# One tuned transformer block on one core: wider loads, a sigmoid from exp and ln, and a maximum subtracted on another engine

## Chip, cores, metric

The kernel runs on one NeuronCore of a Trainium2 chip. The metric is the device time of one execution in microseconds (us). Each kernel is executed several times; the median is quoted, with the lowest and highest run. One execution of each kernel is profiled; its span is some 2 us shorter than its device time.

Every run also lists the mean clock that was granted to TensorE. In this case that column matters: 0.993 of full speed over a span of some 244 us means one stretch of 3.4 us at half clock (3.4 x 0.5 / 244 = 0.7%), as in the profiled run of before (clock 0.50 from 27.69 to 31.10 us), 0.986 two of them. I call such a stretch a **slow window**, and a run with 0.998 or more a **full-clock run**. A run's state, fast or slow, goes by its time. All means below are of runs of state fast; three runs of before that counted as slow (247.36, 248.15 and 249.84 us, at a mean clock of 0.985, 0.978 and 0.972) are left out.

## The reference

A block with adaptive layer norm: six modulation vectors from silu(c), a sliding-window attention (32 heads of 16, eight keys at distance 0, 2, ... 14), and a gated feed-forward.

```python
mod = silu(c) @ w_mod                      # c: 1x512, w_mod: 512x3072 -> sa, ca, ga, sb, cb, gb
h = layernorm(x) * (1 + ca) + sa           # x: 2048x512, bf16
q, k, v = split(h @ wqkv)                  # 512x1536
logits = einsum(q, k[idx]) * Dh**-0.5      # idx = pos - 2*(0..7); masked below 0
o = softmax(logits) @ v[idx]
x = x + ga * (o @ wo)
h = layernorm(x) * (1 + cb) + sb
x = x + gb * ((gelu(h @ w_gate) * (h @ w_up)) @ w_down)     # Df = 1792
```

## The kernel before

The tokens go in five groups (256, 256, 512, 512, 512). Each group has a first normalization, the q, k, v projections, the attention and the feed-forward. The program does not list its instructions in their final order. It declares operations with an engine, an assumed duration, tiles read and written, and a priority; a plan then simulates the engines and fixes the order of every engine. A change of one assumed duration or of one dependence can therefore move instructions that have nothing to do with it.

```python
def start(o):                              # in the plan: can o be placed yet?
    at = max([p.end - ... for p in o.pre], default=0.0)
    for t in o.tiles:
        if t.tag is not None and t not in seen:
            before = self.seqs[t.seq][t.at - 1] if t.at else None
            if before is not None and before not in seen and before not in o.tiles:
                return None                # the tile ahead in the sequence has not been placed
            ...                            # cut
```

The parts that the change touches (cut, in the kernel's own words):

```python
early = T("hh", [P, 2, SG], BF16, "early", "early")
wide = T("hh", [P, 2, SG], BF16, "wide", "early")       # same sequence as wm2 below
...
wm01 = [T("vR", [P, 4, 2, D // 2], BF16, "wm01", "early") for _ in range(2)]
wm2 = [T("hh", [P, 2, D], BF16, "wm2", "early") for _ in range(2)]
...
load_x(0, 2, -1000)
load_wm01(0)                               # shift and scale, 4 loads of 256 KB, rows of 512 B
load_wm01(1)
load_wqkv(0, -998.65)                      # wq, wk, wv: two loads each
load_wqkv(1, -997.5)
load_wqkv(2, L["wv"])
...
act(0.2, lambda: nc.scalar.activation(out=scT[:], in_=c_ps[:], func=ACT.Silu), r=[c_ps], w=[scT], pri=-990,
    table="silu")
dve(0.34, lambda: nc.vector.tensor_copy(out=wide.t[:, 0, :]..., in_=_ap(scT[:], [[1, 4], [0, P]])),
    r=[scT], w=[(wide, 0)], pri=-950)      # "the spread copy": silu(c) over 512 columns
...
if not onact:                              # inverse root of a group's variance: VectorE add, GpSimd power
    dve(0.09, lambda ...: nc.vector.tensor_scalar_add(out=rstd[:], in0=mv[:, :, 1], scalar1=EPS), ...)
    invsqrt(rstd, p)
elif g:                                    # or Ln and Exp on ScalarE, for groups in LNACT = (0, 1)
    act(0.45, lambda ...: rsqrt_act(rstd[:], mv[:, :, 1]), r=[mv, eps1], w=[rstd], pri=p - 1000, table="exp")
...
dve(us, ... Lb[:, 0, :] = max(Lb[:, 0, :], Lb[:, 1, :]))           # maximum over the eight keys
dve(us, ... Lb[0:64, 1, :] = max(Lb[0:64, 0, :], Lb[64:128, 0, :]))
dve(us, ... Lb[0:32, 0, :] = max(Lb[0:32, 1, :], Lb[32:64, 1, :]))
def sub_max():                             # TensorE adds -max to the logits in PSUM
    for t in LT:
        nc.tensor.matmul(t[:], lhsT=NB[:], rhs=_ap(Lb[:, 0, :], [[0, 2 // nb], [1, n]]), start=False, stop=True, ...)
pe(MM * nb, sub_max, r=[NB, Lb], w=LT, pri=p)
```

Of the kernel before, what the change touches and what calls it, by code (L numbers as in the profile page):

```python
# [9 lines left out]
ALU = mybir.AluOpType  # L10
# [188 lines left out]
LNACT = (0, 1)  # L199
SECOND = ()  # L200
MERGE = (3, 4)
FMERGE = 0
CUT = 384
# [26 lines left out]
def kernel(  # L230
# [59 lines left out]
    eps1 = ctile([P, 1], F32, "eps1")  # L290
    M = ctile([P, H], BF16, "Mph")
# [24 lines left out]
    def consts_dve():  # L316
        nc.vector.memset(warm(), 0.0)
        nc.vector.memset(one1[:], 1.0)
        nc.vector.memset(neghalf[:], -0.5)
        nc.vector.memset(onecol[:], 1.0)  # L320
        nc.vector.memset(eps1[:], EPS)

# [29 lines left out]
    dve(0.6, consts_dve, w=[(early, 0), one1, neghalf, onecol, eps1], pri=-1000)  # L352
# [26 lines left out]
    wm01 = [T("vR", [P, 4, 2, D // 2], BF16, "wm01", "early") for _ in range(2)]  # L379
# [32 lines left out]
    def load_wm01(i):  # L412
        for half in range(2):
            lo = half * D + i * (D // 2)
            dma(262e3, lambda half=half, lo=lo: nc.sync.dma_start(  # L415
                out=wm01[i][:, :, half, :], in_=w_mod[:, lo:lo + D // 2].rearrange("(t p) n -> p t n", p=P)),
                w=[(wm01[i], half)], pri=-999 + 0.5 * i + 0.1 * half, bw=385e3)

    def load_wqkv(b, p):
        for i in range(2):  # L420
            dma(262e3, lambda i=i: nc.sync.dma_start(
                out=wqkv[b][:, 2 * i:2 * i + 2, :],
                in_=A_wqkv[2 * i * P:2 * (i + 1) * P, b * D:(b + 1) * D].rearrange("(o p) n -> p o n", o=2)),
                w=[(wqkv[b], k) for k in range(2 * i, 2 * i + 2)], pri=p + 0.25 * i)

    load_wm01(0)
    load_wm01(1)
# [33 lines left out]
    def c_cols():  # L461
        for t in range(4):
# [5 lines left out]
    act(0.2, lambda: nc.scalar.activation(out=scT[:], in_=c_ps[:], func=ACT.Silu), r=[c_ps], w=[scT], pri=-990,  # L468
        table="silu")
    dve(0.34, lambda: nc.vector.tensor_copy(out=wide.t[:, 0, :].rearrange("p (t n) -> p t n", n=P),  # L470
                                            in_=_ap(scT[:], [[1, 4], [0, P]])), r=[scT], w=[(wide, 0)], pri=-950)
# [19 lines left out]
    def mod_first(src, p, after):  # L491
        parts = []
        for i2, chs in enumerate(((0, 1), (2, 3))):
# [4 lines left out]
            def cols(n=n, mps=mps, src=src[i2]):  # L498
                for half in range(2):
                    for i in range(n):  # L500
                        col = mps[:, half * n + i:half * n + i + 1]
                        for kt in range(4):
                            nc.tensor.matmul(col, lhsT=src[:, kt, half, i * P:(i + 1) * P],
# [4 lines left out]
            pe(0.25 * n, cols, r=[src[i2], scT, ident, onecol] + (after if i2 else []), w=[mps], pri=p)  # L508
# [95 lines left out]
    def ln1(g, dst, p):  # L604
        xns = []
        tok0, n = GROUPS[g]
        for half in range(n // 256):
# [7 lines left out]
            for i in range(2):  # L615
                dve(0.6, lambda i=i, st=st, tok=tok: nc.vector.bn_stats(out=st[:, i, :], in_=xrow(tok + P * i)),  # L616
                    r=[xkey(tok + P * i)], w=[(st, i)], pri=p)
                dve(0.081, lambda i=i, st=st, mv=mv: nc.vector.bn_aggr(out=mv[:, i, :], in_=st[:, i, :]),
                    r=[(st, i)], w=[(mv, i)], pri=p)
# [86 lines left out]
    def emit_attention(g):  # L706
# [78 lines left out]
        for b in range(nb):  # L785
# [5 lines left out]
        dve(us, lambda: nc.vector.tensor_tensor(out=Lb[0:64, 1, :], in0=Lb[0:64, 0, :], in1=Lb[64:128, 0, :],  # L791
                                                op=ALU.max), r=[Lb], w=[Lb], pri=p)
        dve(us, lambda: nc.vector.tensor_tensor(out=Lb[0:32, 0, :], in0=Lb[0:32, 1, :], in1=Lb[32:64, 1, :],
                                                op=ALU.max), r=[Lb], w=[Lb], pri=p)

        def sub_max():
            for t in LT:
                nc.tensor.matmul(t[:], lhsT=NB[:], rhs=_ap(Lb[:, 0, :], [[0, 2 // nb], [1, n]]), start=False, stop=True,  # L798
                                 skip_group_check=True)
# [209 lines left out]
```

## Time and profile before

| | before |
|---|---|
| median of the first 3 runs | 246.07 us (245.77 to 246.77) |
| span of the profiled run | 243.9 us, mean clock 0.993 |
| TensorE busy | 235.2 us, 96% |

In the profile, PE is TensorE, PEld its weight loads, DVE VectorE, ACT ScalarE, POOL GpSimd, SPq the queue of SyncE, which issues the loads. A line of a timeline has start, duration, engine, source line, operation, output and inputs, the count of merged instructions, and in brackets the idle time just before with what ended it. The prediction below shows the lines of before.

```profile
5.27 1.32 SPq L421 DMA_DIRECT2D wk<-in_A_wqkv_dram  x2
6.64 1.36 SPq L397 DMA_DIRECT2D wm<-in_w_mod_dram  x2
8.05 1.62 SPq L421 DMA_DIRECT2D wv<-in_A_wqkv_dram  x2
10.05 2.06 SPq L374 DMA_DIRECT2D x_sg<-in_A_x_dram  x3
```

The third part of the modulation weights (wm, 512 KB, not needed before 16 us) goes ahead of wv and of the rows of the later groups.

```profile
17.15 2.46 DVE L616 BATCH_NORM_STATS2 st<-x_sg 128x6 f32<-128x512 bf16 x4
...
22.25 0.72 DVE L532 TENSOR_SCALAR xn<-x_sg,mv,rstd 128x512 bf16<-128x512 bf16 x2
```

### The profile page before, as it was taken

The page shows a single profiled execution, that of the slowest core. Times are in us where ns is not written, and L with a number is a line of the kernel's source. Part 1 is how long each engine was busy: PE and PEld are TensorE (multiplying, and loading weights), DVE is VectorE, ACT ScalarE, POOL GpSimd, SP SyncE. Part 2 cuts the span into 40 slices and gives each one's busy share as a digit, 9 for nine tenths or more (in the row PEclk, how much of TensorE's full clock was granted, in tenths as well). Part 3 has the DMA queues.
Part 4 walks back from the last instruction along what each step waited for, and adds up shares of the span by engine and source line. Part 5 has one row for each costly group of instructions (what it writes and reads, how often), then busy time and mean ns, then how long its engine had stood idle before and what let it go on. Part 6 is the DMA issues. An engine that isn't in the chain of part 4 may idle for free.

```text
span 243.9 us, 4176 instructions
## 1 busy us (share of the span) xinstructions
PE 235.2 (96%) x1572; PEld 126.6 (52%) x1590; DVE 158.5 (65%) x302; ACT 159.5 (65%) x293; POOL 14.8 (6%) x37
## 2 busy tenths in 40 slices
PE   7899699999999999999999999999999999999994
PEld 2688355557665446755444444444444444444443
DVE  3589949829999499993699896299356222222222
ACT  5295687689788769388967748745767902666400
POOL 7002220010001000020000002000002000000000
PEclk9999799999999999999999999999999999999999
DMA  6999999999940309804117602210004010100011
GB/s 179 363 360 304 310 248 379 218 306 209 213 84 6 80 7 256 177 11 79 43 32 187 134 0 55 56 43 26 0 1 81 8 36 7 43 0 3 0 43 43
DMA packets 36533, 28.23 MB, mean 116 GB/s; under 512 B 11041, under 2 KB 35362, under 8 KB 36514
## 3 DMA queue, kind: packets, MB, share of 16 engines
q1 hardware_dynamic: 36512, 27.97, 45.8%
q8 instruction: 12, 0.20, 0.3%
q14 instruction: 7, 0.06, 0.1%
q10 hardware_dynamic: 2, 0.00, 0.0%
HBM read 21.40 MB, written 4.21 MB: 105 GB/s over the span
## 4 chain that ended last, share of the span: by engine, by line
PE 87%; DVE 6%; DMA 2%; ACT 2%; SPq 1%; issue 1%; DVEq 0%
PE g_ps L919 20%; PE u_ps L919 20%; PE y_ps L945 19%; PE qkv_ps L673 14%; PE x_ps L878 6%; PE o_ps L853 3%; PE LT L768 3%; DMA wm<-in_w_mod_dram 2%; DVE st L616 2%; DVE pq L756 2%; ACT hT L547 1%; PE LT L798 1%; PE ss L813 1%; SPq L415 1%; DVE x_sg L953 1%
## 5 line engine op out<-in xcount | busy, mean ns | idle before, releaser
L919 PE MATMUL g_ps<-h2T,Wg 128*128 128x512 bf16 (+1 forms) x280 | 57.7, 337 | 0.0
L919 PE MATMUL u_ps<-h2T,Wu 128*128 128x512 bf16 (+1 forms) x280 | 57.7, 337 | 0.0
L945 PE MATMUL y_ps<-WdP,hht 128*128 128x512 bf16 (+2 forms) x230 | 50.1, 366 | 0.4
L928 ACT ACTIVATE gl<-g_ps 128x512 bf16<-128x512 f32 x56 | 33.6, 600 | 25.6 <-PE g_ps L919 19.8
L932 DVE TENSOR_TENSOR hht<-gl,ub 128x512 bf16<-128x512 bf16 x56 | 23.2, 420 | 33.0 <-ACT ub L931 32.7
L931 ACT CAST ub<-u_ps 128x512 bf16<-128x512 f32 x56 | 32.8, 586 | 14.9 <-PE u_ps L919 14.8
L919 PEld LDWEIGHTS <-Wg 128*128 128x128 bf16 x280 | 27.1, 98 | 23.3 <-issue 1.7
L919 PEld LDWEIGHTS <-Wu 128*128 128x128 bf16 x280 | 27.1, 98 | 22.1 <-issue 1.5
L756 DVE TENSOR_TENSOR pq<-qT,kT 128x2048 bf16<-128x2048 bf16 x32 | 37.5, 1215 | 0.1
L945 PEld LDWEIGHTS <-hht 128*128 128x128 bf16 x238 | 22.8, 98 | 25.7
L953 DVE TENSOR_TENSOR x_sg<-y_ps,x_sg 128x512 bf16<-128x512 f32 (+2 forms) x17 | 10.8, 657 | 29.1 <-PE y_ps L945 29.1
L834 DVE TENSOR_TENSOR pv<-e,vR 128x2048 bf16<-128x2048 bf16 x24 | 28.3, 1217 | 0.1
L537 POOL TENSOR_TENSOR rstd<-rstd,neghalf 128x2 f32<-128x2 f32 x14 | 10.5, 756 | 169.8 <-DVE rstd L893 108.5
L673 PE MATMUL qkv_ps<-hT,wq 128*128 128x512 bf16 (+1 forms) x79 | 17.0, 348 | 0.2
L673 PE MATMUL qkv_ps<-hT,wk 128*128 128x512 bf16 (+1 forms) x78 | 16.8, 346 | 0.2 <-issue 0.2
L673 PE MATMUL qkv_ps<-hT,wv 128*128 128x512 bf16 (+1 forms) x79 | 15.2, 337 | 0.2 <-DMA wv<-in_A_wqkv_dram 0.2
L878 PE MATMUL x_ps<-woP,oT 128*128 128x512 bf16 x60 | 14.6, 379 | 0.2
L885 ACT ACTIVATE xn<-x_sg 128x512 bf16<-128x512 bf16 x16 | 10.0, 630 | 5.9 <-DVE x_sg L882 5.6
L696 ACT CAST kT<-qkv_ps 128x512 bf16<-128x512 f32 x16 | 9.4, 591 | 4.7 <-PE qkv_ps L673 3.6
L673 PEld LDWEIGHTS <-wq 128*128 128x128 bf16 x80 | 8.7, 115 | 6.8 <-issue 2.9
L616 DVE BATCH_NORM_STATS2 st<-x_sg 128x6 f32<-128x512 bf16 x16 | 10.4, 678 | 2.6 <-DMA x_sg<-in_A_x_dram 2.6
L696 ACT CAST qT<-qkv_ps 128x512 bf16<-128x512 f32 x16 | 9.4, 592 | 3.9 <-PE qkv_ps L673 3.7
(92 smaller groups left out, 215.6 us busy)
## 6 DMA issues: line engine op xcount, KB each, us to landing
vR<-scr SPq DMA_DIRECT2D x24, 260.0 KB, 4.9
vR<-scr SPq DMA_DIRECT2D x8, 264.0 KB, 9.5
wm<-in_w_mod_dram SPq DMA_DIRECT2D x8, 256.0 KB, 6.0
out_dram<-x_sg SPq DMA_DIRECT2D x15, 128.0 KB, 1.7
Wg<-in_B_w_gate_dram SPq DMA_DIRECT2D x2, 896.0 KB, 10.0
scr<-vT SPq DMA_DIRECT2D x7, 256.0 KB, 7.1
Wu<-in_B_w_up_dram SPq DMA_DIRECT2D x2, 896.0 KB, 8.5
WdP<-in_B_w_down_dram SPq DMA_DIRECT2D x2, 896.0 KB, 9.9
```

What stands on the lines that cost most here:

```text
L616: dve(0.6, lambda i=i, st=st, tok=tok: nc.vector.bn_stats(out=st[:, i, :], in_=xrow(tok + P * i)), r=[xkey(tok + P * i)], w=[(st, i)], pri=p)
L673: nc.tensor.matmul(shaped(ps[:, jl, :], g, XB1), lhsT=wqkv[b][:, dt, j + jl:D:4], rhs=columns(hT[g], g, dt, XB1), start=(dt == 0 and (jl = ...
L696: act(act_us(SG), lambda dst=dst, ps=ps: nc.scalar.copy(out=dst(), in_=ps[:]), r=[ps], w=w, pri=p)
L756: dve(1.145, lambda j=j, wg=wg, no=no, t=pq[m]: nc.vector.tensor_tensor(out=t[:], in0=_ap(q[g][:, j, :], [[0, no], [1, n]]), in1=_ap(kT[:, ...
L834: dve(1.145, lambda jj=jj, jl=jl, wg=wg, t=pv[m]: nc.vector.tensor_tensor(out=t[:], in0=_ap(e[:, wg, :], [[0, 4], [1, n]]), in1=vR[g][jj][ ...
L878: nc.tensor.matmul(x1_ps[:], lhsT=oT[:, j, c4 * P:(c4 + 1) * P], rhs=woP[:, j, :], start=(j == 0), stop=(j == 3))
L919: nc.tensor.matmul(shaped(ps[:, f, :], g, XB2), lhsT=Wt[:, dt, ft * P:(ft + 1) * P], rhs=columns(h2[g], g, dt, XB2), start=(dt == 0), stop ...
L928: act(act_us(SG), lambda gl=gl, ps=gu[0]: nc.scalar.activation(out=gl[:], in_=flat(ps), func=ACT.Gelu_apprx_tanh), r=[gu[0]], w=[gl], pri= ...
L931: act(act_us(SG), lambda ub=ub, ps=gu[1]: nc.scalar.copy(out=ub[:], in_=flat(ps)), r=[gu[1]], w=[ub], pri=p)
L932: dve(0.339, lambda gl=gl, ub=ub, ht=hh[u // 2], u=u: nc.vector.tensor_tensor(out=ht[:, u % 2, :], in0=gl[:], in1=ub[:], op=ALU.mult), r=[ ...
L945: nc.tensor.matmul(y_ps[:], lhsT=hh[u // 2][:, u % 2, f * n + c4 * P:f * n + (c4 + 1) * P], rhs=WdP[:, ft, lo_d:hi_d], start=(ft == 0), st ...
L953: dve(0.07 + nd * 1.041e-3, lambda y_row=y_row, y_ps=y_ps: nc.vector.tensor_tensor(out=y_row(), in0=y_ps[:], in1=y_row(), op=ALU.add), r=[ ...
```

## The change

Its intent: the first projection waits for the shift and scale weights, so they come in one load with rows four times as long; wq, wk and wv come in one load each; silu is computed from exp and ln, which share one activation table with the inverse roots; the first tiles' statistics are aggregated at once; group 2's inverse root moves to ScalarE; the last group's maximum is subtracted by VectorE instead of TensorE. The spread copy (silu(c) over 512 columns) moves behind the first hT tile. Cut to its core:

```diff
-LNACT = (0, 1)
+LNACT = (0, 1, 2)
+DVEMAX = (4,)
 ...
-    wm01 = [T("vR", [P, 4, 2, D // 2], BF16, "wm01", "early") for _ in range(2)]
+    wm01 = T("vR", [P, 4, 2 * D], BF16, "wm01", "early")
 ...
-    def load_wm01(i): ...                 # four loads, cut
+    dma(1049e3, lambda: nc.sync.dma_start(out=wm01[:], in_=w_mod[:, 0:2 * D].rearrange("(t p) n -> p t n", p=P)),
+        w=[wm01], pri=-999, bw=390e3)
     def load_wqkv(b, p):
-        for i in range(2):
-            dma(262e3, ...)                # cut
+        dma(524e3, lambda: nc.sync.dma_start(
+            out=wqkv[b][:], in_=A_wqkv[:, b * D:(b + 1) * D].rearrange("(o p) n -> p o n", p=P)), w=[wqkv[b]], pri=p)
 ...
-    act(0.2, lambda: nc.scalar.activation(out=scT[:], in_=c_ps[:], func=ACT.Silu), r=[c_ps], w=[scT], pri=-990,
-        table="silu")
-    dve(0.34, lambda: nc.vector.tensor_copy(out=wide.t[:, 0, :]..., in_=_ap(scT[:], ...)), r=[scT], w=[(wide, 0)], pri=-950)
+    def sigmoid():
+        nc.scalar.activation(out=sig[:], in_=c_ps[:], func=ACT.Exp, scale=-1.0)
+        nc.scalar.activation(out=sig[:], in_=sig[:], func=ACT.Ln, bias=one128[:])
+        nc.scalar.activation(out=sig[:], in_=sig[:], func=ACT.Exp, scale=-1.0)
+    act(0.5, sigmoid, r=[c_ps, one128], w=[sig], pri=-990, table="exp")
+    dve(0.15, lambda: nc.vector.tensor_tensor(out=scT[:], in0=c_ps[:], in1=sig[:], op=ALU.mult), ...)
 ...
+                if g == 0:                 # statistics and aggregation as one operation
+                    dve(0.75, lambda stats=stats, aggr=aggr: (stats(), aggr()), ...)
 ...
+        if g in DVEMAX:
+            dve(us, lambda: most(top[0:64, :], Lb[0:64, 0, :], Lb[64:128, 0, :]), ...)
+            dve(4 * us, spread, r=[top], w=[all4], pri=p)      # the last step four times, once for each 32 partitions
+            for b, t in enumerate(LT):
+                dve(..., lambda t=t: nc.vector.tensor_tensor(out=t[:], in0=t[:], in1=_ap(all4[:], ...), op=ALU.subtract), ...)
 ...
         if g == 0:
             mod_keep(mod0, -969)
+            dve(0.34, lambda: nc.vector.tensor_copy(out=wide.t[:, 0, :]..., in_=_ap(scT[:], ...)), r=[scT, hT[0]], w=[(wide, 0)],
+                pri=-950)
```

More of the change, by code (lines that the diff above doesn't have):

```diff
@@ L290 @@
     eps1 = ctile([P, 1], F32, "eps1")
+    one128 = ctile([P, 1], F32, "one128")
     M = ctile([P, H], BF16, "Mph")
@@ L321, in consts_dve @@
         nc.vector.memset(eps1[:], EPS)
+        nc.vector.memset(one128[:], 1.0)
     def consts_ident():
@@ L350, in consts_late @@
                                     fill=NEG, base=-8 * wg - 6, channel_multiplier=2)
-    dve(0.6, consts_dve, w=[(early, 0), one1, neghalf, onecol, eps1], pri=-1000)
+    dve(0.6, consts_dve, w=[(early, 0), one1, neghalf, onecol, eps1, one128], pri=-1000)
     gp(1.0, consts_ident, w=[ident], pri=-1000)
@@ L410 @@
     load_x(0, 2, -1000)
-    def load_wm01(i):
-        for half in range(2):
-            lo = half * D + i * (D // 2)
-            dma(262e3, lambda half=half, lo=lo: nc.sync.dma_start(
-                out=wm01[i][:, :, half, :], in_=w_mod[:, lo:lo + D // 2].rearrange("(t p) n -> p t n", p=P)),
-                w=[(wm01[i], half)], pri=-999 + 0.5 * i + 0.1 * half, bw=385e3)
-    def load_wqkv(b, p):
-        for i in range(2):
-            dma(262e3, lambda i=i: nc.sync.dma_start(
-                out=wqkv[b][:, 2 * i:2 * i + 2, :],
-                in_=A_wqkv[2 * i * P:2 * (i + 1) * P, b * D:(b + 1) * D].rearrange("(o p) n -> p o n", o=2)),
-                w=[(wqkv[b], k) for k in range(2 * i, 2 * i + 2)], pri=p + 0.25 * i)
-    load_wm01(0)
-    load_wm01(1)
+    dma(1049e3, lambda: nc.sync.dma_start(out=wm01[:], in_=w_mod[:, 0:2 * D].rearrange("(t p) n -> p t n", p=P)),
+        w=[wm01], pri=-999, bw=390e3)
+    def load_wqkv(b, p):
+        dma(524e3, lambda: nc.sync.dma_start(
+            out=wqkv[b][:], in_=A_wqkv[:, b * D:(b + 1) * D].rearrange("(o p) n -> p o n", p=P)), w=[wqkv[b]], pri=p)
     load_wqkv(0, -998.65)
@@ L467 @@
     keep_warm(PRI["warm"][1], [c_ps], -989)
-    act(0.2, lambda: nc.scalar.activation(out=scT[:], in_=c_ps[:], func=ACT.Silu), r=[c_ps], w=[scT], pri=-990,
-        table="silu")
-    dve(0.34, lambda: nc.vector.tensor_copy(out=wide.t[:, 0, :].rearrange("p (t n) -> p t n", n=P),
-                                            in_=_ap(scT[:], [[1, 4], [0, P]])), r=[scT], w=[(wide, 0)], pri=-950)
+    sig = ctile([P, 4], F32, "sig")
+    def sigmoid():
[3 more added lines that the diff above has]
+    act(0.5, sigmoid, r=[c_ps, one128], w=[sig], pri=-990, table="exp")
+    dve(0.15, lambda: nc.vector.tensor_tensor(out=scT[:], in0=c_ps[:], in1=sig[:], op=ALU.mult), r=[c_ps, sig],
+        w=[scT], pri=-2000)
     def mod_cols(src0, k0, src1, k1, p, off):
@@ L496, in mod_first, with cols @@
             mps = T("psB", [P, 2 * n], F32, "modT_ps", "mod")
-            def cols(n=n, mps=mps, src=src[i2]):
+            def cols(n=n, mps=mps, first=chs[0] * P):
                 for half in range(2):
@@ L502, in cols @@
                         for kt in range(4):
-                            nc.tensor.matmul(col, lhsT=src[:, kt, half, i * P:(i + 1) * P],
+                            nc.tensor.matmul(col, lhsT=src[:, kt, half * D + first + i * P:half * D + first + (i + 1) * P],
                                              rhs=scT[:, kt:kt + 1], start=(kt == 0), stop=(kt == 3 and half == 0))
@@ L506, in cols @@
                             nc.tensor.matmul(col, lhsT=ident[:], rhs=onecol[:], start=False, stop=True)
-            pe(0.25 * n, cols, r=[src[i2], scT, ident, onecol] + (after if i2 else []), w=[mps], pri=p)
+            pe(0.25 * n, cols, r=[src, scT, ident, onecol] + (after if i2 else []), w=[mps], pri=p)
             parts.append((chs[0], n, mps))
@@ L615, in ln1 @@
             for i in range(2):
-                dve(0.6, lambda i=i, st=st, tok=tok: nc.vector.bn_stats(out=st[:, i, :], in_=xrow(tok + P * i)),
-                    r=[xkey(tok + P * i)], w=[(st, i)], pri=p)
-                dve(0.081, lambda i=i, st=st, mv=mv: nc.vector.bn_aggr(out=mv[:, i, :], in_=st[:, i, :]),
-                    r=[(st, i)], w=[(mv, i)], pri=p)
+                stats = lambda i=i, st=st, tok=tok: nc.vector.bn_stats(out=st[:, i, :], in_=xrow(tok + P * i))
+                aggr = lambda i=i, st=st, mv=mv: nc.vector.bn_aggr(out=mv[:, i, :], in_=st[:, i, :])
+                if g == 0:
+                    dve(0.75, lambda stats=stats, aggr=aggr: (stats(), aggr()), r=[xkey(tok + P * i)],
+                        w=[(st, i), (mv, i)], pri=p)
+                else:
+                    dve(0.6, stats, r=[xkey(tok + P * i)], w=[(st, i)], pri=p)
+                    dve(0.081, aggr, r=[(st, i)], w=[(mv, i)], pri=p)
                 if onact and g == 0:
@@ L790, in emit_attention, with most, spread, sub_max @@
             r=[Lb], w=[Lb], pri=p)
-        dve(us, lambda: nc.vector.tensor_tensor(out=Lb[0:64, 1, :], in0=Lb[0:64, 0, :], in1=Lb[64:128, 0, :],
-                                                op=ALU.max), r=[Lb], w=[Lb], pri=p)
-        dve(us, lambda: nc.vector.tensor_tensor(out=Lb[0:32, 0, :], in0=Lb[0:32, 1, :], in1=Lb[32:64, 1, :],
-                                                op=ALU.max), r=[Lb], w=[Lb], pri=p)
-        def sub_max():
-            for t in LT:
-                nc.tensor.matmul(t[:], lhsT=NB[:], rhs=_ap(Lb[:, 0, :], [[0, 2 // nb], [1, n]]), start=False, stop=True,
-                                 skip_group_check=True)
-        pe(MM * nb, sub_max, r=[NB, Lb], w=LT, pri=p)
+        if g in DVEMAX:
+            mx = [T("ub", [P, n], BF16, "mx") for _ in range(2)]
+            top, all4 = mx
+            def most(out, a, b):
+                nc.vector.tensor_tensor(out=out, in0=a, in1=b, op=ALU.max)
+            def spread():
+                for r in range(4):
+                    most(all4[32 * r:32 * r + 32, :], top[0:32, :], top[32:64, :])
+            dve(us, lambda: most(top[0:64, :], Lb[0:64, 0, :], Lb[64:128, 0, :]), r=[Lb], w=[top], pri=p)
+            dve(4 * us, spread, r=[top], w=[all4], pri=p)
+            for b, t in enumerate(LT):
+                dve(0.072 + SG * 2 // nb * 1.041e-3, lambda t=t: nc.vector.tensor_tensor(
+                    out=t[:], in0=t[:], in1=_ap(all4[:], [[0, 2 // nb], [1, n]]), op=ALU.subtract), r=[t, all4], w=[t],
+                    pri=p)
+        else:
+            dve(us, lambda: nc.vector.tensor_tensor(out=Lb[0:64, 1, :], in0=Lb[0:64, 0, :], in1=Lb[64:128, 0, :],
+                                                    op=ALU.max), r=[Lb], w=[Lb], pri=p)
+            dve(us, lambda: nc.vector.tensor_tensor(out=Lb[0:32, 0, :], in0=Lb[0:32, 1, :], in1=Lb[32:64, 1, :],
+                                                    op=ALU.max), r=[Lb], w=[Lb], pri=p)
+            def sub_max():
+                for t in LT:
+                    nc.tensor.matmul(t[:], lhsT=NB[:], rhs=_ap(Lb[:, 0, :], [[0, 2 // nb], [1, n]]), start=False,
+                                     stop=True, skip_group_check=True)
+            pe(MM * nb, sub_max, r=[NB, Lb], w=LT, pri=p)
         def exps():
@@ L964 @@
             mod_keep(mod0, -969)
+            dve(0.34, lambda: nc.vector.tensor_copy(out=wide.t[:, 0, :].rearrange("p (t n) -> p t n", n=P),
+                                                    in_=_ap(scT[:], [[1, 4], [0, P]])), r=[scT, hT[0]], w=[(wide, 0)],
+                pri=-950)
         emit_qkv(g)
```

## The prediction

> **What bounds the kernel now.** I read the page's busy table and its chain that ended last first, then a table of busy time by stage, then the timeline of each engine in the first 60 us, then the waits. The kernel takes 246.07 us; the profiled span is 243.9 us, so some 2.1 us lie outside the span and I carry them along unchanged. From the page:
>
> ```profile
> PE 235.2 (96%) x1572; PEld 126.6 (52%) x1590; DVE 158.5 (65%) x302; ACT 159.5 (65%) x293; POOL 14.8 (6%) x37
> ...
> PE 87%; DVE 6%; DMA 2%; ACT 2%; SPq 1%; issue 1%; DVEq 0%
> ```
>
> The TensorE (PE) is busy 96% of the span and makes 87% of the chain. So whatever is to be won is either PE work that goes away, or one of the few places where PE waits or runs slowly. The table by stage says where those are (columns: the stretch, its length, then busy time and number of instructions of PE, weight loads, VectorE, ScalarE, GpSimd, then granted clock, DMA share, GB/s):
>
> ```profile
> 0.00:9.59 9.59, 7.15 (x60) 3.30 (x61) 3.74 (x14) 3.85 (x9) 4.36 (x23) 1.00 0.81 241
> 9.59:13.73 4.14, 4.14 (x43) 3.59 (x40) 2.99 (x8) 2.42 (x8) 0.00 (x0) 1.00 1.07 375
> 13.73:27.36 13.63, 11.57 (x155) 10.14 (x155) 13.57 (x35) 10.62 (x20) 2.73 (x4) 1.00 1.07 330
> 27.36:57.00 29.64, 29.16 (x202) 15.99 (x206) 20.77 (x41) 22.84 (x46) 2.27 (x4) 0.94 1.14 282
> 57.00:120.00 63.00, 62.74 (x490) 38.81 (x494) 53.23 (x87) 50.79 (x90) 2.39 (x3) 1.00 0.50 104
> 120.00:200.00 80.00, 79.74 (x436) 35.64 (x440) 54.07 (x99) 52.45 (x96) 3.09 (x4) 1.00 0.22 50
> ```
>
> From 57 us on, PE idles 0.26 us in each of two long stretches: nothing to win there but PE work itself. The head up to the first projection (9.59 us) is not bound by PE: its busy time there is mostly the dummy matmuls[...]. From 13.73 to 27.36 VectorE is the bound (13.57 of 13.63 us busy) and PE idles 2.06 us. In the next stage the mean granted clock is 0.94. So three places: the head, one gap, one slow clock. The timeline of PE shows the head's wait and the gap:
>
> ```profile
> 9.33 0.25 PE L503 MATMUL modT_ps<-scT,wm 128*128 128x1 bf16 x4 [1.18 <-DMA wm<-in_w_mod_dram]
> ...
> 11.50 1.67 PEld L673 LDWEIGHTS <-wk 128*128 128x128 bf16 x16 [0.26 <-DMA wk<-in_A_wqkv_dram]
> ...
> 27.36 0.38 PE L798 MATMUL LT<-Lb,NB 128*128 128x512 bf16 x1 [1.72 <-DVE Lb L793]
> 27.57 1.79 PE L673 MATMUL qkv_ps<-hT,wq 128*128 128x512 bf16 x4
> ```
>
> The second half of the shift/scale weights lands only at about 9.3 us. wk then lands just as it is needed, at 11.5. The last line shows four 512-column matmuls taking 1.79 us where other such groups of four take 1.03: quarter-microsecond windows put the clock at 0.50 from 27.7 to 31.1 us (3.4 us), right after the 1.72 us gap. PE is busy for 3.2 of those 3.4 us, so they cost some 1.6 us of PE time.
>
> [...]the slow stretch is 3.4 us. The window before it (24.3 to 27.7) held PE idle for about half. [...] tensor_tensor[...] 0.41 to 0.43 us for 512 bf16 elements, 0.69 with a PSUM operand. [...]In the trace's packet records a 512 B packet has a median of 27 ns, 1024 B 46 ns, 3584 B 144 ns; over 16 engines that is 303, 356 and 398 GB/s.
>
> **The change, part by part.**
>
> (1) One wide load of shift and scale. Four loads of 256 KB with 512 B rows become one of 1 MB with 2 KB rows. At 303 GB/s the 1049 KB take 3.46 us; at an estimated 385 (between the 1024 B and 3584 B rates above) 2.72: **0.74 us saved**, for everything queued behind them as well. The second half also no longer queues behind half of wq. First data move at about 2.1 us; 262 KB of x and 1049 KB at some 340 GB/s end at about 6[...]: landing near 6.8 instead of 9.3. Then come the column matmuls (0.5 us for each half), the transposes of the first tile (0.6), and the first of the four hT writes (0.75 for two): PE can start q at about 8.3, if wq is there. The queue has delivered 1835 KB, x to wq, by about 7.5, landing near 8.3. So q begins about 1.2 us earlier. But then wk bounds: it came at 11.5 and moves only by the queue's saving, to some 10.7. I take **0.8 us** for the head.
>
> (2) wq, wk, wv in one load each. The SyncE issues fewer loads (0.5 us each), but the DMA engines have over 1.0 share from 5.5 us on, so issue was not the limit. The first matmul must wait for all of wq instead of its first half. Value 0.
>
> (3) Silu from exp, ln, exp. A table load at 4.00 (1.28 us) goes; three small activations (0.2 to 0.3 each, as the rstd lines) and one multiply replace one of 0.17. The first tile is normalized (5.86 to 6.7) before the weights land, and PE's dummy matmuls run to 6.9 anyway. Value 0. The same holds for statistics and aggregation done at once in the first tile (4), and for the copy that spreads scT (0.39 us), moved to a time when VectorE idles.
>
> (5) Group 2's inverse root on ScalarE. Two VectorE additions (0.15 us) and two GpSimd powers (0.69 each) become two pairs of activations (about 0.5 a pair). The aggregates of both halves are done at 19.89, yet the normalization starts at 22.25 and 23.49: the addition waits behind a product (20.92), GpSimd ends at 21.9. With ScalarE it could start right after the product, at 21.0, and the second half follows at once: 1.2 to 2 us earlier. VectorE fills the time with statistics of later groups, so its own sum hardly falls; but hT of group 2 comes earlier, and with it PE work for the gap. That stage is exp-only on ScalarE (the gelu table comes at 57.33), so no table switch. I take the 1.72 us gap down to about 0.8: **0.9 us**. [...]1.6 us with a chance of 0.6, **1.0 us**.
>
> (6) The last group's maximum on VectorE. Two 512-column matmuls go: the chain shows them as 0.43 us in the saturated part, **0.43 us** gained. VectorE: one of the three max steps (0.41) becomes four (1.4 in a row), and two subtractions in PSUM are added (0.69 each): 0.33 x 3 + 1.3 = 2.3 us more. It idles 3.94 us at 152 to 156, and PE has the down projection of another group to do, so exp comes about 1 us later without harm.
>
> Sum: 0.8 + 0.9 + 1.0 + 0.43 = 3.1. The order of all instructions is planned from assumed durations, so every change reshuffles it; I take off 0.4 for that. 246.07 - 2.7, rounded: **243.3 us**.
>
> **Rivals.** *The queue binds anyway*: nearly everything in the head waits on bytes, and those stay the same. For: wk and wv landed just when needed, and from 8.5 to 13 us the queue already moves 370 to 387 GB/s. Against: between 4 and 5 us it moves only 158 to 209. If wide rows are no faster, only 0.2 of the head remains: about 243.9. *VectorE stays the bound of 13 to 27 us*: it is busy 13.57 of 13.63 us and the change takes 0.15 from it. If the reordering of group 2 does not feed PE, gap and slow clock stay: 246.07 - 0.8 - 0.43, about 244.9. *VectorE in the last group*: 2.3 us more, and two of the three buffers of the up-projection's copy are lent to the maxima; if exp then comes late enough for PE to run out of other work, 0.43 becomes a loss of 0.5 to 1: about 244.4. Against it: PE runs 30 us of feed-forward after 160 us that does not need this group. *All goes well*: gap and slow clock vanish (1.7 + 1.6), head 1.2, sub 0.43: 241.1, just over 2%.
>
> **Range and chances.** The rivals span 241.1 to 244.9; a bad reshuffle can add a microsecond. I set 241.5 to 245.3. Faster by over 2% means below 241.15, which needs every part at its best: 0.07. Slower by over 2% would need 5 us lost in a saturated kernel: 0.01. Within 2%: 0.92.
>
> **What would show each step right or wrong.** The shift/scale load should land near 7 us, 2 KB packets should run at over 370 GB/s, q's first matmul should start at 8.2 to 8.8 and wk's at about 10.7. One table load less on ScalarE before 6 us, and no shift of the first projection by it. Group 2's normalization should start 1 to 2 us earlier; PE's idle between its first projection and 30 us should fall from 2 us to about 1; no 0.50 clock after it. Two matmuls of the subtraction should be missing near 153 us, with PE still without gaps from 57 us on. I am wrong if the gap moves elsewhere, if the slow clock appears at another place, or if a table switch enters the stage after 57 us through group 2.

## The result

The kernel after takes 242.81 us in the median of 4 runs (242.07 to 243.28); before has 245.92 us in the same rounds (244.86 to 246.77). The ratio is 0.9873, with a 95% interval of 0.9825 to 0.992. Ratios here are the mean time of one kernel's fast runs over that of the other's fast runs of the same rounds, so not quite the ratio of the medians. The outputs are correct.

Later runs allow a wider pool. Before ran in three later jobs with 30 fast runs, mean 245.48 (the four runs of the first job are not among them); after has 10, the four above and six on another chip (ratio there 0.9944, interval 0.9892 to 0.9994), mean 243.30. The difference of these means is 2.2 us. It mixes chips: in the first job the means differ by 3.1 us (245.87 and 242.74), in the one later job that ran both kernels by 1.4 (245.05 and 243.68).

The page of after:

```profile
PE 233.4 (97%) x1573; PEld 126.7 (53%) x1591; DVE 160.7 (67%) x307; ACT 159.0 (66%) x298; POOL 13.1 (5%) x35
...
PE 83%; DMA 10%; DVE 2%; SPq 2%; ACT 1%; issue 1%; DVEq 0%
```

The same stretches as before in the table by stage:

```profile
0.00:9.59 9.59, 8.27 (x71) 4.68 (x72) 4.40 (x18) 3.32 (x12) 4.08 (x23) 1.00 0.82 275
9.59:13.73 4.14, 3.89 (x41) 3.62 (x39) 3.17 (x8) 2.62 (x8) 0.00 (x0) 1.00 1.10 348
13.73:27.36 13.63, 13.27 (x158) 10.63 (x158) 13.48 (x34) 11.81 (x26) 1.37 (x2) 1.00 1.07 361
27.36:57.00 29.64, 28.11 (x212) 16.45 (x216) 22.70 (x42) 24.28 (x47) 2.19 (x3) 1.00 1.16 278
```

TensorE's idle time from 13.73 to 27.36 has fallen from 2.06 to 0.36 us, and no clock below 1.00 is left in this profile. From 27.36 to 57 it idles 1.53 us, where before idled 0.48: a part is given back. TensorE's timeline:

```profile
7.36 0.44 PE L503 MATMUL modT_ps<-scT,wm 128*128 128x1 bf16 x12
...
8.47 1.91 PE L677 MATMUL qkv_ps<-hT,wq 128*128 128x256 bf16 x16
10.62 1.94 PE L677 MATMUL qkv_ps<-hT,wk 128*128 128x256 bf16 x16 [0.25 <-DMA wk<-in_A_wqkv_dram]
...
27.43 0.38 PE L820 MATMUL LT<-Lb,NB 128*128 128x512 bf16 x1 [0.15 <-DVE Lb L815]
...
53.32 1.04 PE L941 MATMUL g_ps<-h2T,Wg 128*128 128x256 bf16 x8
```

q starts at 8.47 instead of 9.59, wk at 10.62 instead of 11.51. The first group's subtraction comes no earlier (27.43 against 27.36): VectorE, busy 13.48 of 13.63 us, sets it. But TensorE now has projections of group 2 to do before it, and so waits 0.15 instead of 1.72 us. The first gate matmul stands at 53.32; before has it at 56.18 in the same view. That is 2.9 us, all of the difference of the two spans (243.9 and 240.7) but 0.4. By an estimate 1.6 us of it are the stretch at half clock that only before's profile has (3.19 us busy at 0.50). VectorE shows where the early projections come from:

```profile
13.99 2.46 DVE L616 BATCH_NORM_STATS2 st<-x_sg 128x6 f32<-128x512 bf16 x4
...
17.76 1.38 DVE L532 TENSOR_SCALAR xn<-x_sg,mv,rstd 128x512 bf16<-128x512 bf16 x4
```

Group 2's statistics start 3.2 us earlier and its normalization 4.5 us. I had predicted 1.2 to 2. The order of the loads has changed as well:

```profile
3.51 0.57 SPq L419 DMA_DIRECT2D wv<-in_A_wqkv_dram  x1
...
4.13 3.51 SPq L377 DMA_DIRECT2D x_sg<-in_A_x_dram  x2
...
7.68 2.48 SPq L400 DMA_DIRECT2D wm<-in_w_mod_dram  x2
```

wv and group 2's rows now overtake the third part of the modulation weights. Nothing in the loads' priorities was changed. This was not in my prediction, and it became the main question.

### The profile page after: what moved, and what is told of

It reads as the page before. It is cut to its first block, busy times and chain, and to the rows that moved or that the text cites.

```text
span 240.7 us, 4178 instructions
## 1 busy us (share of the span) xinstructions
PE 233.4 (97%) x1573; PEld 126.7 (53%) x1591; DVE 160.7 (67%) x307; ACT 159.0 (66%) x298; POOL 13.1 (5%) x35
## 4 chain that ended last, share of the span: by engine, by line
PE 83%; DMA 10%; DVE 2%; SPq 2%; ACT 1%; issue 1%; DVEq 0%
PE u_ps L941 20%; PE g_ps L941 20%; PE y_ps L967 19%; PE qkv_ps L677 9%; PE x_ps L900 6%; DMA vR<-scr 4%; DMA wk<-in_A_wqkv_dram 3%; PE o_ps L875 3%; DMA scr<-vT 3%; PE LT L772 3%; DVE pv L862 2%; ACT hT L547 1%; SPq L721 1%; PE ss L835 1%; DVE x_sg L975 1%
## 5 line engine op out<-in xcount | busy, mean ns | idle before, releaser
L975 DVE TENSOR_TENSOR x_sg<-y_ps,x_sg 128x512 bf16<-128x512 f32 (+2 forms) x17 | 10.8, 656 | 26.6 <-PE y_ps L967 26.6
L537 POOL TENSOR_TENSOR rstd<-rstd,neghalf 128x2 f32<-128x2 f32 x12 | 9.0, 756 | 170.0 <-DVE rstd L915 107.5
L677 PE MATMUL qkv_ps<-hT,wk 128*128 128x512 bf16 (+1 forms) x79 | 16.3, 337 | 0.9 <-ACT hT L547 0.6
L677 PE MATMUL qkv_ps<-hT,wq 128*128 128x512 bf16 (+1 forms) x78 | 16.2, 335 | 0.5 <-issue 0.2
L677 PEld LDWEIGHTS <-wk 128*128 128x128 bf16 x80 | 8.7, 114 | 5.8 <-issue 1.1
```

The costliest lines, as they stand in the source:

```text
L677: nc.tensor.matmul(shaped(ps[:, jl, :], g, XB1), lhsT=wqkv[b][:, dt, j + jl:D:4], rhs=columns(hT[g], g, dt, XB1), start=(dt == 0 and (jl = ...
L975: dve(0.07 + nd * 1.041e-3, lambda y_row=y_row, y_ps=y_ps: nc.vector.tensor_tensor(out=y_row(), in0=y_ps[:], in1=y_row(), op=ALU.add), r=[ ...
```

## The experiments

Twelve kernels were run; all gave correct results. In names that end in "same_order" the plan is fed exactly what it was fed in its base kernel, and only the emitted instructions differ. The lists of instructions of all engines were compared with the base: apart from the exchanged instructions they are identical. This separates what an operation costs from what the plan does with it. e5_gap_filled keeps the order of before as well. The other versions are planned anew.

| run | base | mean of fast runs | full-clock runs (mean) | ratio to before, same job (95%) |
|---|---|---|---|---|
| e1_wide_only | before | 245.36 | 3 of 6 (245.63) | 0.9994 (0.9944 to 1.0044) |
| e2_rsqrt2_only | before | 245.60 | 1 of 6 (244.98) | 1.0003 (0.9956 to 1.0051) |
| e2f_rsqrt2_same_order | before | 244.84 | 3 of 6 (244.32) | 0.9972 (0.9925 to 1.0020) |
| e5_gap_filled | before | 245.63 | 4 of 6 (245.11) | 0.9993 (0.9941 to 1.0044) |
| x1_copy_early | after | 244.71 | 6 of 6 (244.71) | 0.9964 (0.9934 to 0.9994) |
| x2_copy_late_only | before | 247.87 | 1 of 6 (247.78) | 1.0093 (1.0058 to 1.0127) |
| e6f_pool_rsqrt2_same_order | after | 243.66 | 6 of 6 (243.66) | 0.9921 (0.9888 to 0.9954) |
| e3f_no_dvemax_same_order | after | 244.22 | 7 of 8 (243.91) | 0.9922 (0.9888 to 0.9955) |
| after_again | after | 243.68 | 5 of 6 (243.25) | 0.9943 (0.9892 to 0.9994) |
| e7f_narrow_rows_same_order | after | 245.13 | 2 of 6 (245.74) | 1.0002 (0.9958 to 1.0047) |
| e4f_table_loads_same_order | after | 244.64 | 2 of 6 (242.81) | 0.9983 (0.9923 to 1.0042) |
| i5_max_roots_same_order | after | 245.29 | 2 of 6 (244.27) | 1.0018 (0.9964 to 1.0071) |
| before, three jobs | | 245.48 (30 runs) | 11 of 30 (244.52) | |
| after, with the first four | | 243.30 (10 runs) | 9 of 10 (243.03) | |

Lines of four run together (e1 to e5, x1 to e3f, after_again to i5) share a chip. The full-clock mean of before was 244.35, 245.02 and 244.31 on the three chips (3 or 4 runs each), so differences of 0.7 us between jobs are not resolved.

The runs of before give the price of a slow window without any experiment: 11 full-clock runs have a mean of 244.52, 12 runs with one window 245.48, 7 with two 246.99. One costs 1.0 us, two 2.5 (0.4 to 1.4 and 1.9 to 2.8 on the single chips). A caution: the mean clock does not count the first microseconds. In before the records of the clock begin, at full clock, at 7.21 us (in after at 7.18), and the clock column says 1.00 ahead of that too. Yet the first dummy matmuls there take 0.43 us each for 512 columns (five in 2.32 us; later ones need 0.22), and seven from 3.70 us on take 3.17 us, as in after. In x1 four of them, from 4.67 us on, take 1.03. The profiled runs of after and x1 both have a mean clock of 1.000, so this difference does not show in it.

### Wide load alone

```diff
 # before, with only
+    dma(1049e3, lambda: nc.sync.dma_start(out=wm01[:], in_=w_mod[:, 0:2 * D].rearrange("(t p) n -> p t n", p=P)), w=[wm01], ...)
 # in place of the four loads, and the matching lhsT slices
```

> The kernel before with one part of the change alone: shift and scale in one load with 2 KB rows. VectorE's order stays that of before. Theory: q's first matmul at about 8.5 us instead of 9.6, wk's at about 10.7 instead of 11.5, and the 0.8 us pass down the VectorE-bound stage to the end: about 245.1 where before has 245.9; PE's gap ahead of the subtraction of the first group and the slow clock stay. Rival: the stage of VectorE up to 27 us absorbs it, and the time is that of before within 0.3 us.

TensorE's timeline of this run:

```profile
8.61 1.91 PE L667 MATMUL qkv_ps<-hT,wq 128*128 128x256 bf16 x16
10.35 1.91 PE L667 MATMUL qkv_ps<-hT,wk 128*128 128x256 bf16 x16
...
26.21 0.39 PE L792 MATMUL LT<-Lb,NB 128*128 128x512 bf16 x1 [2.32 <-DVE Lb L787]
...
64.06 1.95 PE L872 MATMUL x_ps<-woP,oT 128*128 128x512 bf16 x7 [0.65 <-ACT oT L853]
```

The head is as fast as in after, and VectorE's chain moves with it: the subtraction comes 1.15 us earlier than before's 27.36. But TensorE's gap grows to 2.32 us, and a new wait of 0.65 us stands at 64 us in the new order. The time is that of before within 0.5%. That interval would still hold a gain of 0.8 us, but the three full-clock runs (244.84, 245.14 and 246.9) are all slower than the four of before (243.88 to 244.74). So the head alone shows no gain at the end; my expectation of 0.8 us failed.

### Group 2's root alone, planned anew and in the old order

```diff
-LNACT = (0, 1)
+LNACT = (0, 1, 2)
```

> The kernel before with one part alone: group 2's inverse root on ScalarE, planned anew. Theory: group 2's normalization comes 2 us or more earlier, its projections fill PE's 1.7 us gap, the clock is not halved at 27.7 us; 1.5 to 2.5 us gained, about 243.9. Rival: the gap is closed only by the earlier head; then 0.2 us at most, about 245.7, and the slow clock stays.

```profile
26.45 0.39 PE L798 MATMUL LT<-Lb,NB 128*128 128x512 bf16 x1 [2.13 <-DVE Lb L793]
26.68 1.05 PE L673 MATMUL qkv_ps<-hT,wq 128*128 128x512 bf16 x4
```

ScalarE's timeline of the same run, for what those projections need:

```profile
23.79 2.80 ACT L547 ACTIVATE hT<-tp,modT,scl 128x512 bf16<-128x512 bf16 x4
```

The normalization does come 2.1 us earlier (20.10). Some 0.8 us of that are a head that happened to be faster in this profile (group 2's statistics start at 16.33, not 17.15), so the root's own share is about 1.3, within the 1.2 to 2 that I had reckoned. The gap stays all the same, at 2.13 us, and so do the slow windows (5 of 6 runs). The reason stands in the second line: ScalarE writes hT from 23.79 to 26.6 us, so the projections cannot start ahead of the subtraction at 26.45. In after it writes the first two of four hT tiles from 20.84. The normalization is not what holds hT back there: the first transpose for it starts at 21.52, but in ScalarE's order hT stands behind the casts of vT and Lb (22.83 and 23.31), and ScalarE idles 1.45 us before the first of these. So by this profile it is the order that keeps the gap.

In the old order, with ScalarE doing the work at GpSimd's place:

```diff
-                dve(0.09, add EPS, ...)
-                invsqrt(rstd, p)
+                dve(0.09, (lambda: None) if g == 2 else add, ...)
+                gp(0.75, lambda ...: rsqrt_act(rstd[:], mv[:, :, 1]), ...)      # emitted on ScalarE for group 2
```

> The kernel before with group 2's inverse root on ScalarE, but with every engine's instruction order held as it was before (the plan still believes that GpSimd does it). Theory: the gain lies in the order that the plan can choose, not in the shorter operation; the normalization of group 2 still stands behind two statistics, at about 22.1 us, and gap and slow clock stay: at most 0.4 us gained, about 245.6. Rival: the operation's own latency counts, and the time falls as in the re-planned version, by over 1 us.

It gains 0.7 us in the mean (244.84 against 245.57), but the interval includes 1, at full clock the two are equal (244.32 and 244.35), and the gap stays at 1.96 us. It is no slower than the re-planned version, so for this part alone the plan's freedom was worth nothing. My expectation, that most of what the root buys comes through the order, finds no support in this; the two intervals overlap, so it is not refuted either.

### The gap filled with dummies

```diff
         def sub_max():
+            if g == 0:
+                filler(ss.t, 12)          # 12 matmuls of 256 columns into a PSUM tile that is overwritten later
             for t in LT:
```

> The kernel before, all orders kept, with twelve 256-column dummy matmuls (1.3 us of PE) put into PE's gap ahead of the first group's maximum subtraction. Theory: the slow clock from 27.7 to 31.1 us follows from that gap and costs 1.6 us on the path; the clock stays 1.0 and the time falls by about 1.5 us, to 244.4, though the gap brings no useful work. Rival: PE waits for others in that stretch anyway; the clock is full but the time falls by less than 0.5 us. Second rival: the slow clock does not come from the gap and stays.

The mean is 245.63, against 245.57 for before; 4 of 6 runs had full clock (4 of 11 for before). In the profiled run two slow windows, one behind the other, stand in the head. Two stretches of the table by stage:

```profile
6.10:9.50 3.40, 1.58 (x38) 1.24 (x37) 1.33 (x4) 0.36 (x3) 0.00 (x0) 0.89 1.08 354
9.50:12.90 3.40, 3.40 (x26) 2.42 (x27) 2.25 (x6) 0.24 (x3) 0.00 (x0) 0.50 1.09 383
```

The 0.89 of the first line says that the half clock began inside it: by these shares (the next 3.5 us have 0.62) it lasted from about 8.75 to 15.6 us. In the 3.4 us before it TensorE was busy some 2.0 us (it waited for the shift and scale weights, 0.80 and 0.60 us). The profile of before shows half clock at the other place: in the 3.4 us from 24.28 to 27.69 TensorE was busy 1.61 us, and the clock was 0.50 for the next 3.4. So half clock came behind the waits of the head in one profile and behind the gap in the other, and filling the gap leaves the head as it was. Both expectations were too simple; that the dummies lower the time is not shown. A gap does not always bring a slow window: e1 and x1 show gaps of 2.32 and 1.51 us in profiles whose clock is 1.00 in every stage up to 235 us.

The length of a wait does not tell the cases apart. In e2f TensorE waited 1.96 us ahead of the subtraction (28.55), and the clock was 1.00 in every stage from 13.73 us on. In its head no wait from 5 us on was longer than 0.56 us (ahead of 8.35), and yet q's projection, from 9.40 on, took 3.18 us where before took 1.92, with a mean clock of 0.59 from 9.59 to 13.73. What decides whether half clock follows was not shown.

### The spread copy

The list of loads suggested a cause that I had valued at zero. The third part of the modulation weights lies in tiles (wm2) that stand behind `wide` in one sequence. Tiles of one sequence take their buffers in the order of declaration, so in the plan they cannot be loaded until `wide` has its first use, which is the spread copy. With the copy early they are free at once; with the copy behind the first hT they are held back until then, and wv and group 2's rows go first. To test it, the copy alone was put back in after, and moved alone in before.

```diff
 # x1, against after: the copy at its old place
+    dve(0.34, lambda: nc.vector.tensor_copy(out=wide.t[:, 0, :]..., ...), r=[scT], w=[(wide, 0)], pri=-950)
 ...
-            dve(0.34, lambda: nc.vector.tensor_copy(out=wide.t[:, 0, :]..., ...), r=[scT, hT[0]], w=[(wide, 0)], pri=-950)
 # x2, against before: the same lines the other way round
```

> The kernel after with one thing undone: the copy that spreads silu(c) over 512 columns comes early again instead of behind the first hT. New theory: this copy is what holds the third part of the modulation weights (512 KB) back in the plan; with it early these loads go ahead of wv and of group 2's rows again, group 2's statistics come some 2.5 us later, PE's gap near 26 us returns (over 1.2 us), and slow-clock windows return in some runs: about 244.5, full-clock runs about 243.8. Rival: the copy is only moved into idle time of VectorE; time and gap stay as after, about 242.8.

The loads of x1, from SyncE's timeline, then its waits on TensorE:

```profile
3.44 1.24 SPq L400 DMA_DIRECT2D wm<-in_w_mod_dram  x2
4.72 1.68 SPq L419 DMA_DIRECT2D wv<-in_A_wqkv_dram  x1
6.45 4.67 SPq L377 DMA_DIRECT2D x_sg<-in_A_x_dram  x3
```

```profile
13.66 1.50 PE L680 MATMUL qkv_ps<-hT,wv 128*128 128x256 bf16 x12 [0.39 <-DMA wv<-in_A_wqkv_dram]
...
26.05 0.39 PE L823 MATMUL LT<-Lb,NB 128*128 128x512 bf16 x1 [1.51 <-DVE Lb L818]
...
64.22 1.96 PE L903 MATMUL x_ps<-woP,oT 128*128 128x512 bf16 x8 [0.95 <-ACT oT L884]
```

The old order of loads is back, group 2's statistics start at 16.53 instead of 13.99, TensorE's gap is 1.51 us, wv is waited for, and 0.95 us are lost at 64 us. All six runs lie between 244.50 and 244.91. That is 1.05 us above e6f of the same job (243.66, none of its six runs above 244.46), which is after with another part undone, and 0.8 above e3f at full clock (243.91). After itself did not run in this job. At full clock x1 is 0.31 us below before of its job, after_again 1.06 below before of its own. So without the moved copy most of the gain at full clock is gone. The new theory holds for after in this, with one limit: x1 is planned anew, and not only the loads changed. Group 2's first rows land at 15.13 us instead of 13.59, yet the statistics start only at 16.53: the plan put two more products ahead of them on VectorE, which did not wait for the rows. So later rows account for at most 1.5 of the 2.5 us, and what the loads alone are worth, with VectorE's order held, no run shows. Its second half, that slow windows return, failed: none of the six runs had one.

> The kernel before with only this copy moved behind the first hT. New theory: wv and group 2's rows overtake the 512 KB of modulation weights, statistics of group 2 start near 15 us instead of 17.15, the gap near 26 us falls below 1 us: about 244.3 (before 245.6), and fewer slow windows. Rival: the late head (q at 9.6) and GpSimd's root keep the gap; time as before within 0.3 us.

This failed clearly: 247.87, slower than before by 0.9%, and five of six runs with slow windows. The loads do change their order as expected (wv at 7.29 us, straight behind wk). But the statistics start only at 16.96, TensorE's gap ahead of the subtraction is 2.09 us, and the first gate matmul comes at 58.17. In the profiled run q's projection takes 3.27 us at half clock, and the second group's normalization waits 1.93 us for ScalarE. Group 2's first rows did land 1.5 us earlier (15.02 instead of 16.50), but VectorE came late to them: two products, begun at 14.68, stood ahead of the statistics. The single run with 0.998 also took 247.78, so slow windows are not the whole of it. What else in its order costs 2 us I did not take apart. Alone the copy's move did not pay; what it is worth shows only together with the rest of the change.

### Group 2's root, in the order of after

```diff
-                act(0.45, lambda ...: rsqrt_act(rstd[:], mv[:, :, 1]), ...)
+                act(0.45, on_pool if g == 2 else ..., ...)      # emitted: VectorE addition, GpSimd power
```

> The kernel after, every engine's order kept, but group 2's inverse root by a VectorE addition and a GpSimd power again. Theory: a product of 1.19 us lies between aggregates and normalization in this order and hides GpSimd's 0.69 us; the time stays at 242.8 to 243.1. Rival: the latency of GpSimd is on the path and the time rises by 0.7 us or more.

```profile
17.66 0.23 DVE L633 TENSOR_SCALAR rstd<-mv 128x2 f32<-128x2 f32 x2
...
18.65 1.54 DVE L532 TENSOR_SCALAR xn<-x_sg,mv,rstd 128x512 bf16<-128x512 bf16 x4 [0.76 <-POOL rstd L634]
```

The rival was right about the mechanism: the addition stands behind the product in VectorE's order (17.66, the product at 16.55), so the product hides nothing, and VectorE waits 0.76 us for GpSimd. It delays the subtraction from 27.43 to 28.47. The time is 243.66, 0.6 above after's pooled full-clock mean, but the two were not run on one chip, and chips differ by as much. Shown is the wait, not its price at the end.

### The last group's maximum

```diff
-                dve(..., lambda t=t: nc.vector.tensor_tensor(out=t[:], in0=t[:], in1=..., op=ALU.subtract), ...)
+                dve(..., lambda t=t: nc.tensor.matmul(t[:], lhsT=NB[:], rhs=..., start=False, stop=True), ...)
```

> The kernel after, all orders kept, with the last group's maximum subtracted by two matmuls again (they stand in PE's order where the subtraction stood). Theory: PE is full there, so its two 512-column matmuls cost 0.43 us: 243.2, with PE still without gaps from 57 us on. Rival: the end of that group is bound by the path to its exponentials, which becomes 1 us shorter; then the time is that of after or less.

```profile
150.29 4.48 PE L966 MATMUL y_ps<-WdP,hht 128*128 128x512 bf16 x20
154.60 0.59 PE L808 MATMUL LT<-Lb,NB 128*128 128x512 bf16 x2
155.03 3.62 PE L966 MATMUL y_ps<-WdP,hht 128*128 128x512 bf16 x16
```

The two matmuls hold TensorE from 154.60 to 155.03, 0.43 us, between down projections that follow each other without a gap. In after the same place reads 35 down-projection matmuls in one row. The full-clock mean is 243.91, which is 0.9 above after's pooled mean and so agrees in direction, but again on another chip. Its profiled run (246.35) had a slow window at 42 us (four 512-column matmuls in 1.90 us from 41.89 on), behind waits of 0.56, 0.73 and 0.73 us for VectorE's products; that run is not used for the time.

### After again, narrow rows, table loads

> The kernel after, unchanged, as the reference for the other runs of this job: 242.8 us, nearly all runs at full clock. A theory that slow windows vanish for good expects 0.998 or more in at least five of six runs; one that the four first runs were lucky expects some at 0.993, as before has them.

The median was 243.37, five of six runs at full clock and one at 0.992 (245.81). Slow windows become rare in after, 1 of 10 runs, but do not vanish.

```diff
-    dma(1049e3, lambda: nc.sync.dma_start(out=wm01[:], ...), w=[wm01], ...)
+    dma(1049e3, load_wm01, w=[wm01], ...)     # emits four loads with rows of 512 B, all ahead of wq
```

> The kernel after, all orders kept, but shift and scale in four loads with 512 B rows, all of them ahead of wq. Theory: packets of 512 B run at some 303 GB/s instead of 390, the queue loses 0.74 us and SyncE issues three loads more; q starts near 9.2 us, wk's first matmul near 11.3, and the time is 243.4 or more. Rival: that half of wq stood between the four loads was the whole loss of before, and row size does not count: wk as after, at 10.6, and 242.8.

```profile
9.70 3.51 PE L683 MATMUL qkv_ps<-hT,wq 128*128 128x256 bf16 x16 [1.10 <-DMA wq<-in_A_wqkv_dram]
13.00 2.05 PE L683 MATMUL qkv_ps<-hT,wk 128*128 128x256 bf16 x16
```

The median is 245.11, 1.7 us above after_again of the same job, and four of six runs have a slow window. In the profiled run q starts 1.5 us later than in after_again (8.21) and waits for wq. Then the clock is halved from about 9.9 us, so that q takes 3.51 instead of 1.94 us and wk starts 2.5 us later. Slow windows do not explain the loss, for the two full-clock runs (245.11 and 246.37) are no faster than the others. So having all of these weights ahead of wq is not what gains: with narrow rows in that order, all that after had won over before in this job (245.05 in the mean) is lost again. The difference is not all due to the row length, for three more issues of about 0.5 us each by SyncE (0.45 to 0.52 in before) are part of it. In the packet records a 2 KB packet takes 84 ns in the median, that is 390 GB/s over 16 engines, where I had estimated 385; 512 B packets took 27 ns (303 GB/s) in before. The narrow loads also show a dip that the wide one does not: 182 GB/s from 4.0 to 4.5 us, against 389 in after_again. Before had it at the same place (158). I don't know its cause. (Packets of 1024 B took 46 ns in after, 356 GB/s, and those of 3584 B 142 ns, 404 GB/s.)

```diff
-        nc.scalar.activation(out=sig[:], in_=c_ps[:], func=ACT.Exp, scale=-1.0)       # and Ln, Exp
+        nc.scalar.activation(out=sig[:], in_=c_ps[:], func=ACT.Sigmoid)
+        pl.preload["exp"]()
```

> The kernel after, all orders kept, but the sigmoid by its own activation table, so that a second and a third table load (1.28 us each) come before the first tile's inverse roots. Theory: normalization of the first tile ends 0.5 to 0.8 us later, q's first matmul some 0.4 us later, but wk's arrival at 10.6 takes that up: the time stays within 0.2 us of after. Rival: the first tile is on the path in this order, and the time rises by 0.5 us or more.

```profile
8.79 0.45 PE L502 MATMUL modT_ps<-scT,wm 128*128 128x1 bf16 x12 [1.21 <-DMA wm<-in_w_mod_dram]
```

Two runs at full clock took 242.54 and 243.08, as after. The other four had slow windows, and the median is 245.29. In the profiled run there was one more table load of 1.28 us (at 3.99) than in after, and the next activation started at 5.29, within 0.02 us of its end; the first tile's normalizations ended at 6.7 instead of 6.3 us, still under the dummy matmuls, which run to 6.9. What TensorE waited for was the wide load, 7.4 us from issue to landing where after had 5.5. The table load is not on the path in that profile, and the full-clock runs agree. Whether it has to do with the four slow runs is not settled: I see no link between the table and the load, and six runs are few.

### A version meant to beat both

```diff
+                if g in (2, 3):                # maxima of groups 2 and 3 on VectorE as well
+                    for r in range(4): nc.vector.tensor_tensor(out=mxA.t[32*r:32*r+32, :], ..., op=ALU.max)
+                ...
+                    gp(0.75, lambda ...: rsqrt_act(rstd[:], mv[:, :, 1]), ...)   # roots of groups 3 and 4 on ScalarE
```

> A version meant to beat both: the kernel after, orders kept, with the maxima of groups 2 and 3 subtracted on VectorE as well (four 512-column matmuls less, 0.86 us of a full PE) and the inverse roots of groups 3 and 4 on ScalarE (GpSimd's wait of 0.8 us before a normalization near 31 us goes, which is followed by a PE wait of 0.57 us for hT). Theory: 0.9 to 1.4 us gained, about 241.6. Rival: VectorE or ScalarE, busier between 70 and 115 us, delay the exponentials and PE waits in their place: 242.8 or slower.

```profile
33.59 1.02 PE L681 MATMUL qkv_ps<-hT,wk 128*128 128x512 bf16 x4 [1.41 <-ACT hT L548]
79.72 1.46 PE L985 MATMUL y_ps<-WdP,hht 128*128 128x512 bf16 x6 [1.21 <-DVE WdP L1016]
```

It is slower: 245.29 in the mean, and its two full-clock runs, both 244.27, are 1.0 above the 243.25 of after_again. The first line is the price of the roots: ScalarE is then late with hT, and the wait of 0.57 us became one of 1.41. The second is the price of the maxima: VectorE scales the down-projection weights behind the new subtractions, and TensorE waits 1.21 us for them. So the same exchange that gains 0.43 us of TensorE in the last group, where VectorE idled for 4 us, loses in group 2, where it does not. Both parts went in at once, so these are two waits read in one profile and not two tests. After stands as the best version found.

## Why the prediction was right

The predicted time was 243.3 with a range of 241.5 to 245.3; 242.81 was measured at first and 243.3 in the pool. The range holds both. The steps were less right than the sum, and that the sum fits is in part luck: the head's 0.8 us does not show at the end by itself, and the copy, put at 0, takes back 0.8 to 1.05 us when it is undone. In the one later job that ran both kernels the gain was 1.4 us, half of the 2.7 predicted. (Two small slips: 246.07 - 0.8 - 0.43 is 244.8, not 244.9, and the queue's lowest rate from 8.5 to 13 us is 367 GB/s, not 370.)

**The head was right as an event, but not as a term of the sum.** Landing near 6.8 (6.80 measured: issued at 1.33, 5.5 to landing, the last packet ended at 6.47), q at 8.3 (8.47), wk at 10.7 (10.62), 385 GB/s (390). But "0.8 us for the head" assumed that the end moves with it. The wide load alone moved the mean by 0.2 us (interval some 1.2 us either way), and its full-clock runs were all slower than those of before. In the changed kernel its absence cost 1.7 us of median, three more issues included, and its two full-clock runs were no faster. So the wide load counts in the changed kernel, but the sum's reason for it is not shown.

**The zeros were partly right.** The table load is off the path in the profile and costs nothing in full-clock runs. The loads of wq, wk and wv and the statistics were not tested alone.

**The step that failed is the value 0 for the spread copy**, "moved to a time when VectorE idles". VectorE's 0.39 us was indeed free. But the copy holds a place in a sequence of tiles, and its move reordered 2 MB of loads (wm2 and wv, 0.5 MB each, and 1 MB of rows of x). Undone in the changed kernel, it takes back 1.05 us against e6f and 0.8 against e3f, through the loads and the order that the plan then chooses; the two are not separated.

**The step "ScalarE's root feeds the gap" had the right end and the wrong cause.** The gap closed further than predicted (0.15 us left, not 0.8). But the root alone leaves a gap of 2.13 us, as my second rival had it, for ScalarE's writing of hT comes too late in its order. Only in the order that after plans around earlier rows does the normalization come 4.5 us earlier and the projections in time. There the root and the copy both count: with the root undone the gap is 0.71 us (e6f), with the copy undone 1.51 (x1).

**The slow window was right in kind and too dear.** I put 1.6 us on it; the 30 runs of before give 1.0 for one and 2.5 for two. I gave 0.6 to its going away with a smaller gap, a guess from one profile, and saw only the one behind the gap. In fact 19 of 30 runs of before had one or two windows, 1 of 10 of after; they arise in the head as well. From full-clock means (244.52 and 243.03) some 1.5 of the 2.2 us are order and loads, the rest, 0.7, are slow windows, where I had put 1.0. In the one job that ran both it is 1.1 of 1.4.

**The subtraction was right**: 0.43 us, seen in place in the trace. Its total is too small to be resolved between chips. The reshuffle that I took off 0.4 for is real: 1.05 us more idle from 27 to 57 us.

## What to carry to other kernels

Where a plan orders the instructions, a change has two values: what the operation costs in a fixed order, and what the plan then does with everything else. Test both, with the order held and planned anew, and read the list of loads first: an operation of 0.4 us may be the key that lets megabytes go. Parts that are worth nothing alone can be worth microseconds together, so take them away from the new kernel as well as adding them to the old one. And before differences of half a per cent are explained, sort the runs by clock.
